# A hand-placed gated mixer kernel with a new order of all operations on every engine

## The chip, the cores and the metric

One Trainium2 chip, one core. The metric is device time in microseconds (us) of one launch. The kernel before took 224.87 us, the median of three runs (223.43 to 225.10).

## The reference

Two branches share the input `q` (2048 rows of 640, bf16) and are mixed by a gate per row:

```python
g = sigmoid((x * gate_w).sum(-1))                 # one number per row
k_shift = 4-tap causal filter of k;  kv = k_shift * v
y = causal convolution of kv with ssm_k (length 2048, per channel; by FFT)
a = q * (y + kv * ssm_D)
h  = gelu(layernorm(x) @ w1)                      # 640 -> 640
x1 = x + shift_rows(h) @ w2                       # four column groups shifted by +1, -1, +2, -2 rows
b  = x1 + gelu(layernorm(x1) @ w3) @ w4           # 640 -> 1536 -> 640
out = g * a + (1 - g) * b
```

## The kernel before

The program first records 1176 operations with their operands and memory regions (class `Prog`), and then issues them in an order that is written out by hand as a list. An **operation** here is one instruction of VectorE (DVE), ScalarE (ACT) or GpSimd, one DMA, or one group of matmuls into a PSUM bank; it is named by its number in the recording. Three literals in the main function steer all of it:

- `SEQUENCE` is the order of the 1176 numbers. Each engine takes its own operations in that order, and so does each DMA queue: the queue of SyncE (SP) for loads, stores and transposing DMAs, the queue of GpSimd for DMAs that add into their target.
- `PLACES` gives the PSUM bank of each of the 206 matmul results.
- `ON` is a string of 151 bits. `turn(default)` flips the engine of one operation where its bit is "1": ScalarE or VectorE for copies and scalings, a DMA or VectorE for 32-row copies and for some additions.

`emit` walks the order, and before an operation waits on a semaphore for each operation whose result (or whose memory) it needs, also for an earlier one of the same engine, TensorE apart. Nothing is reordered at run time, so an engine whose next operation isn't ready stands still.

The parts of the work, by the functions that record them:

- `x_load`, `ln1`: load 16 row tiles; mean and variance with two `bn_stats` per tile (L847) and `bn_aggr` (L848); GpSimd raises the variance to the power -0.5 (`pool_pow`, L855); VectorE normalises; TensorE or a transposing DMA turns the tile.
- `mm1`, `mmg`: first matmul with gelu on ScalarE; 32-row pieces are copied to shifted places (L932), 24 in all.
- `mm2`, `ln2`: second matmul; VectorE adds the residual out of PSUM (L966); statistics, the power on GpSimd again, a normalising pass per tile (on ScalarE or VectorE by `turn`), a transposing DMA.
- `mm3`, `base`, `mm4`: the 1536-wide pair of matmuls, in four blocks of 512 rows; its result is added into the output by DMAs on GpSimd's queue.
- For each of five channel chunks c: `h_load`, `h_fold`, `h_even`, `h_chunk` take the filter to its spectrum HF; `k_load`, `v_load`, `kv`, `kv2`, `x_fwd`, `combine` take the signal to XF; `unit` multiplies the two spectra block by block. `unit` is VectorE's largest part: multiplications and additions over 1024 or 2048 elements in each of 128 partitions (L646); fourteen of the additions are done by DMAs that add.
- `final`: inverse transform by matmuls, flip, gating and the last additions.

Helper lines in the profile: L646 is every two-input VectorE operation (`tt`), L651 every one-input one (`ts`), L656 every ScalarE pass (`act`), L678 nearly every matmul (`mm`), L237 and L234 the plain and the transposing DMAs, L852 the small three-input operations. So a row is told apart by its shape.

Of the kernel before, what the change touches and what calls it, by code (L numbers as in the profile page):

```python
# [433 lines left out]
def bass_gated_mix__ssm_conv_h3__mixer_s_mlp__prompt_kernel(  # L434
    nc, A_q, A_k, A_v, A_shift_k, A_ssm_k, A_ssm_D, B_x, B_w1, B_w2, B_w3, B_w4, gate_w, out,
):
    S, D, F = 2048, 640, 1536
# [3 lines left out]
    P = Prog(nc)  # L441
# [27 lines left out]
    def ps(n, cls):  # L469
# [3 lines left out]
    SEQUENCE = [2, 4, 27, 1, 24, 7, 0, 5, 3, 8, 46, 53, 9, 10, 11, 45, 52, 12, 13, 14, 49, 15, 50, 16, 17, 25, 18,  # L473
# [66 lines left out]
    ON = ("0000000011111111111111111011011100110100010000101111000000000000011000000000110100000001010010001101"  # L540
          "001000010100001000100000000000000000000000000000000")
# [608 lines left out]
```

## Time and profile before

| | us |
|---|---|
| three runs | 224.87, 223.43, 225.10 |
| span of the profiled execution, first to last instruction | 222.3 |
| VectorE: first instruction, end of the last one | 0.82, 219.5 |
| last store lands, end of the span | 222.3 |

The profile is of one execution; its span is 1.1 to 2.8 us below the three runs, which also hold what lies around the span. A row of groups gives the line, engine and operation, the shape written and read, the count, then busy time in us and the mean duration of one in ns, then the idle time of the engine just before them. A row of the timeline gives start, length, engine, line, operation and count; the idle time before it, with what ended it, stands in brackets. Starts and lengths of neighbours on VectorE overlap by some 80 ns, so what one instruction costs is less than its duration.

### The profile page before, as it was taken

The numbers are of one execution on the slowest core, as the hardware profiler recorded it, in microseconds if no ns is written. First come the engines' busy times: TensorE is split into PE (matmuls) and PEld (weight loads), VectorE is DVE, ScalarE is ACT, GpSimd is POOL, SyncE is SP. The second block draws the span as 40 slices with busy tenths as digits, with TensorE's granted clock in tenths as the row PEclk, the third lists the DMA queues.
The fourth block names the chain that finished last, engine by engine and source line by source line (L and its number), as shares of the span: only waits on it lengthen the run. The fifth ranks groups of instructions, "written<-read, shape, count | busy, mean of one in ns | idle before, by whom it ended". The sixth has DMA issues, their size and how long they took to land.

```text
span 222.3 us, 3842 instructions
## 1 busy us (share of the span) xinstructions
PE 210.2 (95%) x1403; PEld 125.7 (57%) x1410; DVE 211.8 (95%) x417; ACT 193.4 (87%) x324; POOL 53.5 (24%) x57
## 2 busy tenths in 40 slices
PE   5999989799999999999999999999999999999971
PEld 2588755344675444665445575445666444677650
DVE  6999999899999979999999999999998999999994
ACT  2389999799999999899999999999987698666891
POOL 0422303200003300005140003034015416287431
PEclk9999999999999999999999999999999999999997
DMA  5997999999999999939958874599699959979895
GB/s 166 344 299 181 213 208 246 169 253 190 147 361 212 321 226 172 200 78 189 233 108 146 200 153 94 119 174 184 142 226 138 232 77 265 200 100 96 110 161 112
DMA packets 80561, 41.39 MB, mean 186 GB/s; under 512 B 59129, under 2 KB 77086, under 8 KB 80542
## 3 DMA queue, kind: packets, MB, share of 16 engines
q1 hardware_dynamic: 73872, 31.89, 64.9%
q0 software_dynamic: 6496, 9.18, 26.7%
q8 instruction: 11, 0.18, 0.3%
q10 hardware_dynamic: 174, 0.07, 0.1%
q14 instruction: 8, 0.07, 0.1%
HBM read 14.88 MB, written 5.77 MB: 93 GB/s over the span
## 4 chain that ended last, share of the span: by engine, by line
DVE 65%; PE 13%; ACT 11%; DMA 7%; issue 2%; ACTq 0%
DVE arena L646 59%; ACT arena L656 11%; PE PSall L678 10%; DMA arena<-arena 7%; PE PSall L701 3%; DVE arena L651 2%; DVE arena L932 1%; DVE arena L847 1%; DVE arena L966 1%; PE PSall L908 0%; DVE arena L852 0%; DVE arena L698 0%; DVE arena L848 0%; PE PSall L731 0%; DVE arena L689 0%
## 5 line engine op out<-in xcount | busy, mean ns | idle before, releaser
L678 PE MATMUL PSall<-arena 128*128 128x512 bf16 (+5 forms) x1342 | 202.0, 309 | 4.9 <-DVE arena L646 2.2
L646 DVE TENSOR_TENSOR arena<-arena 128x1024 bf16<-128x1024 bf16 (+13 forms) x266 | 173.4, 712 | 4.1 <-DMA arena<-arena 2.7
L678 PEld LDWEIGHTS PSall<-arena 128*128 128x128 bf16 x1349 | 121.4, 98 | 85.1 <-ACT arena L656 6.7
L656 ACT ACTIVATE arena<-PSall 128x512 bf16<-128x512 f32 (+6 forms) x157 | 93.4, 666 | 10.7 <-PE PSall L736 4.9
L656 ACT ACTIVATE arena<-arena 128x640 bf16<-128x640 bf16 (+5 forms) x105 | 90.7, 892 | 4.5 <-DVE arena L646 4.2
L855 POOL TENSOR_TENSOR arena<-arena 128x2 f32<-128x2 f32 (+2 forms) x15 | 17.1, 1145 | 87.6 <-DVE arena L852 71.4
L237 POOL DMA_DIRECT2D out_dram<-arena x24 | 25.5, 1285 | 15.1 <-DVE arena L646 8.9
L656 ACT ACTIVATE arena<-PSall,arena 128x640 bf16<-128x640 f32 (+2 forms) x32 | 20.4, 655 | 8.5 <-PE PSall L678 8.4
L237 POOL DMA_DIRECT2D arena<-arena x14 | 12.4, 882 | 61.1 <-DVE arena L646 61.1
L966 DVE SCALAR_TENSOR_TENSOR arena<-PSall,arena 128x640 bf16<-128x640 f32 x16 | 12.9, 814 | 0.5 <-PE PSall L678 0.5
L651 DVE TENSOR_SCALAR arena<-arena 128x640 bf16<-128x640 bf16 (+6 forms) x37 | 13.2, 376 | 0.1
L847 DVE BATCH_NORM_STATS2 arena<-arena 128x6 f32<-128x320 bf16 x20 | 8.8, 479 | 1.1 <-DMA arena<-in_A_q_dram 1.0
L701 PE MATMUL PSall<-arena 128*128 128x512 bf16 x15 | 6.4, 586 | 2.2 <-DVE arena L698 2.2
L932 DVE TENSOR_SCALAR arena<-arena 32x256 bf16<-32x256 bf16 (+1 forms) x23 | 5.5, 237 | 0.6 <-ACT arena L656 0.3
L656 ACT ACTIVATION_READ_ACCUMULATOR arena<-arena 128x1 f32 x28 | 5.8, 206 | 0.0
L701 PEld LDWEIGHTS PSall<-arena 128*128 128x128 bf16 x15 | 1.9, 136 | 5.0 <-issue 2.8
L908 PE MATMUL PSall<-arena 128*128 128x128 bf16 x40 | 3.4, 220 | 0.1
L852 DVE SCALAR_TENSOR_TENSOR arena<-arena 128x2 f32<-128x2 f32 (+2 forms) x19 | 3.0, 157 | 0.2 <-ACT arena L656 0.2
L908 PEld LDWEIGHTS PSall<-arena 128*128 128x128 bf16 x40 | 2.5, 98 | 0.5 <-DVE arena L651 0.2
L704 ACT ACT_TABLE_LOAD x1 | 1.3, 1283 | 1.3 <-PEq L1135 1.3
L848 DVE BATCH_NORM_AGGREGATE arena<-arena 128x2 f32<-128x12 f32 x10 | 1.8, 199 | 0.0
L966 DVE DVE_READ_ACCUMULATOR arena<-PSall,arena 128x1 f32 x16 | 1.3, 79 | 0.0
(19 smaller groups left out, 2.9 us busy)
## 6 DMA issues: line engine op xcount, KB each, us to landing
arena<-arena POOLq DMA_DIRECT2D x9, 512.0 KB, 6.5
arena<-in_A_ssm_k_dram SPq DMA_DIRECT2D x5, 512.0 KB, 4.2
arena<-in_A_q_dram SPq DMA_DIRECT2D x6, 320.0 KB, 5.7
arena<-in_B_w_dram SPq DMA_DIRECT2D x1, 1920.0 KB, 10.5
out_dram<-arena SPq DMA_DIRECT2D x16, 96.0 KB, 2.9
out_dram<-arena POOLq DMA_DIRECT2D x16, 96.0 KB, 4.7
arena<-in_A_q_dram SPq DMA_DIRECT2D x8, 192.0 KB, 3.3
out_dram<-arena POOLq DMA_DIRECT2D x8, 192.0 KB, 4.2
```

What stands on the lines that cost most here:

```text
L237: fn = lambda e: e.dma_start(out, in_, **kw)
L646: P.op(eng, lambda e: e.tensor_tensor(o, real(a), real(b), op), [a, b], [o], dve_ns(o, [a, b], 2) if eng == "dve" else 500)
L651: P.op(eng, lambda e: e.tensor_scalar(o, real(a), s1, s2, op0=op0, **({} if op1 is None else {"op1": op1})), [a] + aps, [o], dve_ns(o, [a] ...
L656: P.op("act", lambda e: e.activation(real(o), real(a), f, bias=bias, scale=scale, **({"accum_out": accum} if accum is not None else {})), ...
L678: fns.append(lambda e, l=l, r=r, i=i: e.matmul(real(o), l, r, start=(i == 0), stop=(i == last)))
L701: P.op("pe", lambda e: e.matmul(real(pw), warm[:, 0:128], warm[:, 128:640], start=True, stop=True), [warm], [pw], 427.0 if i < 14 else 216.0)
L847: P.op("dve", lambda e, o=o, i=i: e.bn_stats(o, i), [i], [o], 400)
L852: P.op("dve", lambda e: e.scalar_tensor_tensor(o, a, x, b, op0=op0, op1=op1), [a, b] + aps, [o], n_of(o) / 0.96 + 65)
L855: P.op("pool", lambda g: g.tensor_tensor(o, a, e, ALU.pow), [a, e], [o], dur)
L908: P.op("pe", [lambda e, c=c, pb=pb, xn=xn: e.transpose(real(pb)[:, 128 * c:128 * (c + 1)], xn[:, 128 * c:128 * (c + 1)], ident) for c in r ...
L932: P.op("dve", lambda e, o=hT[q, 4, c0:c0 + n], i=hx[q, :]: e.tensor_scalar(o, i, 1.0, None, op0=ALU.mult), [hx[q, :]], [hT[q, 4, c0:c0 + n ...
L966: P.op("dve", lambda e: e.scalar_tensor_tensor(x, real(pr), 1.0, x, op0=ALU.mult, op1=ALU.add, accum_out=st[1, 0][:, t:t + 1]), [pr, x], [ ...
```

## The change

All three literals are replaced: another `SEQUENCE` of the same 1176 operations, other `PLACES`, and `ON` with eleven bits changed. Two of the small clearing operations (L692, L694) name a wider region as their output in the recording; the instructions stay the same. The note on the change reads: laid out with longer GpSimd powers and later landings. These are figures that the order was worked out with; no such figure is part of the program.

What the eleven bits move (number, part, engine before, engine after):

| operation | before | after |
|---|---|---|
| 301, a filter tap of `kv(0)`, 128x2048 | ACT | DVE |
| 402, a copy of `h_even(2)`, 1x1024 | ACT | DVE |
| 518, 522 (`ln2(0,4)`) and 544, 545, 547 (`ln2(4,8)`), normalising passes, 128x640 | ACT | DVE |
| 129, gate sums of `mmg(0)`, 128x4 | ACT | DVE |
| 269, a 32-row copy of `mm1(3)`, 32x512 | DMA (SP) | DVE |
| 768, an addition of `unit(3)`, 128x2048 | DMA (GpSimd) | DVE |
| 815, a copy of `unit(4)`, 1x512 | DVE | ACT |

Moves of place that the prediction speaks of:

- SP's queue starts 46, 45, 47, 48, 130 before and 46, 45, 47, 130, 48 after (46, 45, 47, 48 load one 160 KB tile of x each, 130 loads two, 320 KB).
- GpSimd's queue has 542 (power of `ln2(4,8)`), 637, 640 (adding DMAs of `unit(0)`) before, and 637, 542, 640 after.
- The copies and additions of `h_even(2)` (400, 402) stand 5 us of VectorE work later, TensorE's `h_chunk(2)` (416, 417) at the same place among the matmuls.

```diff
-    SEQUENCE = [2, 4, 27, 1, 24, 7, 0, 5, 3, 8, 46, 53, 9, 10, 11, 45, 52, 12, 13, 14, 49, 15, 50, 16, 17, 25, 18,
...
+    SEQUENCE = [27, 46, 8, 28, 45, 26, 1, 5, 4, 3, 2, 0, 9, 47, 10, 25, 11, 130, 12, 24, 13, 48, 31, 32, 52, 131,
...
-    ON = ("0000000011111111111111111011011100110100010000101111000000000000011000000000110100000001010010001101"
-          "001000010100001000100000000000000000000000000000000")
+    ON = ("0000000001111111111111111111011110110110010000100110111000000000011000000000110100000001010010001100"
+          "001000010100001000000000000000000000000000000000000")
...
-    P.op("dve", lambda e: e.memset(hT[0:32, 4, 2:3], 0.0), [], [hT[0:32, 4, 2:3]], 70)
+    P.op("dve", lambda e: e.memset(hT[0:32, 4, 2:3], 0.0), [], [hT[0:32, 4, 2:4]], 70)
...
-    P.op("dve", lambda e: e.memset(hT[32:64, 4, S + 1:S + 2], 0.0), [], [hT[32:64, 4, S + 1:S + 2]], 70)
+    P.op("dve", lambda e: e.memset(hT[32:64, 4, S + 1:S + 2], 0.0), [], [hT[32:64, 4, S:S + 2]], 70)
```

More of the change, by code (lines that the diff above doesn't have):

```diff
@@ L471, in ps @@
         return v if n == 1 else v.rearrange("p (b n) -> p b n", b=2)
-    SEQUENCE = [2, 4, 27, 1, 24, 7, 0, 5, 3, 8, 46, 53, 9, 10, 11, 45, 52, 12, 13, 14, 49, 15, 50, 16, 17, 25, 18,
[59 rows of a table removed]
-    PLACES = [2, 4, 7, 0, 4, 5, 6, 1, 2, 1, 3, 4, 2, 3, 3, 4, 2, 6, 7, 2, 0, 4, 5, 7, 6, 2, 6, 1, 0, 7, 4, 1, 6, 0,
[6 rows of a table removed]
-    ON = ("0000000011111111111111111011011100110100010000101111000000000000011000000000110100000001010010001101"
-          "001000010100001000100000000000000000000000000000000")
+    SEQUENCE = [27, 46, 8, 28, 45, 26, 1, 5, 4, 3, 2, 0, 9, 47, 10, 25, 11, 130, 12, 24, 13, 48, 31, 32, 52, 131,
[59 rows of a table added]
+    PLACES = [0, 1, 3, 7, 2, 4, 5, 0, 2, 3, 3, 0, 5, 0, 6, 6, 6, 5, 7, 2, 7, 7, 1, 6, 6, 0, 4, 0, 5, 1, 5, 4, 2, 0,
[6 rows of a table added]
+    ON = ("0000000001111111111111111111011110110110010000100110111000000000011000000000110100000001010010001100"
+          "001000010100001000000000000000000000000000000000000")
     HW = S + 4
```

130 rows, old and new, of tables (PLACES, SEQUENCE) are left out of this document.

## The prediction, made before the result was known

> **What bounds the kernel now.** I read the engines' busy shares first, then the chain of waits that ended last, then the busy time by stretches.
>
> ```profile
> PE 210.2 (95%) x1403; PEld 125.7 (57%) x1410; DVE 211.8 (95%) x417; ACT 193.4 (87%) x324; POOL 53.5 (24%) x57
> ...
> DVE 65%; PE 13%; ACT 11%; DMA 7%; issue 2%; ACTq 0%
> ```
>
> ```profile
> 68.00:86.00 18.00, 17.95 (x88) 8.40 (x88) 16.62 (x25) 17.79 (x25) 3.87 (x3) 1.00 1.04 250
> 86.00:122.00 36.00, 35.85 (x212) 20.54 (x213) 35.93 (x53) 35.06 (x50) 6.65 (x5) 1.00 0.82 159
> 122.00:163.00 41.00, 40.95 (x246) 23.96 (x246) 40.97 (x59) 39.76 (x57) 6.86 (x8) 1.00 0.79 156
> 163.00:207.00 44.00, 43.74 (x272) 26.23 (x271) 42.70 (x62) 33.28 (x56) 21.54 (x24) 1.00 0.97 162
> ```
>
> The columns of the second view are the stretch, its length, and the busy time of TensorE, its weight loads, VectorE, ScalarE and GpSimd. VectorE and TensorE are both nearly full; ScalarE has room only after 163 us. The chain goes through VectorE for 65% of the span. A matmul's end is modelled, so TensorE's 17.95 of 18 may hide small waits; VectorE's gaps are true ones, and these are all that were longer than 0.15 us:
>
> ```profile
> 3.18 1.67 DVE L847 BATCH_NORM_STATS2 arena<-arena 128x6 f32<-128x320 bf16 x4 [1.00 <-DMA arena<-in_A_q_dram]
> 15.21 0.22 DVE L932 TENSOR_SCALAR arena<-arena 32x256 bf16<-32x256 bf16 x1 [0.28 <-ACT arena L656]
> 41.89 0.16 DVE L852 SCALAR_TENSOR_TENSOR arena<-arena 128x4 f32<-128x4 f32 x1 [0.18 <-ACT arena L656]
> 43.22 0.69 DVE L646 TENSOR_TENSOR arena<-arena 128x1024 bf16<-128x1024 bf16 x1 [0.45 <-DMA arena<-arena]
> 52.19 1.31 DVE L646 TENSOR_TENSOR arena<-arena 128x16 f32<-128x16 f32 x2 [0.18 <-ACT arena L656]
> 64.33 0.82 DVE L966 SCALAR_TENSOR_TENSOR arena<-PSall,arena 128x640 bf16<-128x640 f32 x1 [0.53 <-PE PSall L678]
> 67.57 1.23 DVE L646 TENSOR_TENSOR arena<-arena 128x2047 bf16<-128x2047 bf16 x1 [0.45 <-ACT arena L656]
> 82.22 1.55 DVE L646 TENSOR_TENSOR arena<-arena 128x2048 bf16<-128x2048 bf16 x2 [1.38 <-DMA arena<-arena]
> ...
> 170.49 36.72 DVE L646 TENSOR_TENSOR arena<-arena 128x2048 bf16<-128x2048 bf16 x52 [0.89 <-DMA arena<-arena]
> ```
>
> They sum to 5.34 us. So VectorE is the bound: it works almost without a break from 3.2 us to its end, and all that a better order alone can win here is 5.3 us less the first load.
>
> **The change, part by part.** First what VectorE has to do. Of the eleven flipped operations ten come to VectorE and one leaves it. Their prices:
>
> ```profile
> L646 DVE TENSOR_TENSOR arena<-arena 128x2048 bf16<-128x2048 bf16 x56 | 66.8, 1216 | 2.5 <-DMA arena<-arena 2.3
> L651 DVE TENSOR_SCALAR arena<-arena 128x640 bf16<-128x640 bf16 x16 | 6.8, 430 | 0.1
> L651 DVE TENSOR_SCALAR arena<-arena 128x2048 bf16<-128x2048 bf16 x6 | 4.4, 748 | 0.0
> L932 DVE TENSOR_SCALAR arena<-arena 32x512 bf16<-32x512 bf16 x7 | 2.0, 286 | 0.1
> L651 DVE TENSOR_SCALAR arena<-arena 1x512 bf16<-1x512 bf16 x1 | 0.3, 274 | 0.0
> ```
>
> ```profile
> 41.97 0.80 DVE L651 TENSOR_SCALAR arena<-arena 128x640 bf16<-128x640 bf16 x2
> ...
> 48.62 1.41 DVE L651 TENSOR_SCALAR arena<-arena 128x2048 bf16<-128x2048 bf16 x2
> ```
>
> Two taps of 0.75 us take 1.41 together, two normalising passes of 0.44 take 0.80: a neighbour starts 0.08 us before the one in front of it ends, so an instruction costs its duration less 0.08. Operation 301 then costs 0.66; the five normalising passes 5 x 0.36 = 1.78; the addition 768 costs 1.22 - 0.08 = 1.14; the 32-row copy 269 costs 0.29 - 0.08 = 0.21; 815, which leaves, gives back 0.19. Two shapes have no row. The 1x1024 copy lies between the 1x512 copy (0.19) and the full 2048 pass (0.66); I take 0.38, twice the shorter, since it has twice the elements. The four gate sums lie between nothing and 0.25 (they read PSUM, as the 0.81 us additions of L966 do with 640 elements); I take 0.07. Sum: 0.66 + 1.78 + 1.14 + 0.21 + 0.38 + 0.07 - 0.19 = 4.05 us, with bounds 3.8 and 4.6.
>
> An instruction that needs the one just in front of it does not overlap. In the chain of waits such a pair looks like this:
>
> ```profile
> 189.09 0.02 issue
> 189.12 1.24 DVE arena L646
> ```
>
> The start is 0.02 to 0.03 us after the end of the one in front instead of 0.08 before it, so 0.11 us are lost. Counting neighbours in both written orders gives 16 such pairs before and 13 after: 0.35 us less. The 32-row copies break the overlap too; changes between 32-row groups number 36 in both orders, so they add nothing. **VectorE's work grows by 3.7 us.** ScalarE loses eight passes and gains one; on VectorE that can shorten only the four waits on ScalarE above.
>
> The Trainium skill (VectorE: DVE Perf Modes, "The DRAIN you can't avoid") says that a semaphore between two VectorE operations costs nothing extra, because the pipe drains anyway. By that the 0.35 us would not be saved and the sum below would end 0.35 us higher. The rows above differ (0.08 us of overlap without a wait, none with one), and the measurement decides.
>
> Next the loads at the start. Tile 48 now stands behind the 320 KB of 130 on SP's queue.
>
> ```profile
> L237 SPq DMA_DIRECT2D arena<-in_A_q_dram x1: 432/432/432, 2.1 to 2.1; - x1
> ...
> DMA to landing us min/median/max: 4.0/4.0/4.0
> ```
>
> ```profile
> L237 SPq DMA_DIRECT2D arena<-in_A_q_dram x1: 452/452/452, 2.6 to 2.6; - x1
> ...
> DMA to landing us min/median/max: 4.9/4.9/4.9
> ```
>
> 48 landed at 6.1 us, 130 at 7.5. With the two swapped the same bytes have to pass before 48 is there, so it lands at 7.5. On VectorE 48's statistics come after those of tile 47 (landed 5.3, two at 0.42) and two small operations (0.36), at 6.5 us: a wait of 1.0 us. The old order lost 0.1 on 130 there, so this costs 0.9, with bounds 0 (if landings do not follow the queue) and 1.2.
>
> Then the old waits. The 0.89 us at 170 us ended with the adding DMA 768; the addition is now VectorE's own, and is priced above. The 1.38 us at 82.2 ended with the adding DMA 637, which took 8.9 us to land:
>
> ```profile
> 73.33 1.07 POOL L237 DMA_DIRECT2D arena<-arena  x1 [1.72 <-DVE arena L646]
> 77.08 0.88 POOL L237 DMA_DIRECT2D arena<-arena  x1 [2.68 <-DVE arena L646]
> ```
>
> Between the last product that it adds and its reader lay 7.9 us of VectorE work, and now lie 11.8: gone, with 3 us to spare. The matmuls behind the 0.53 at 64.3 stand 4 us earlier on TensorE. The readers behind the waits on ScalarE (0.28, 0.18, 0.18, 0.45) stand 2.7 to 13 us of VectorE work later, while ScalarE has less in front of them. I let these seven go: 3.89 us. The 0.45 at 43.2 stays, since the room before it is 6.38 us and was 6.41; the first load stays.
>
> Last, new waits. Along the new order I added up VectorE's work between each producer and its reader. It is tight in few places: the readers of adding DMAs in `unit(3)` and `unit(4)` have 0.3 and 0.5 us less room than before and would just wait; the powers of the first tiles are read 0.2 us after they should be done. I take 0.6 us for all of it, with bounds 0 and 3.
>
> **Sum**, against the profiled execution: 222.3 + 3.7 + 0.9 - 3.9 + 0.6 = 223.6 us of span, 0.6% more. The runs shown have a median of 224.87 for this span of 222.3; scaled alike the forecast is **226.2 us**. What a measurement of this kernel can tell from no change is about 1%, here 222.6 to 227.1.
>
> **Rivals.**
>
> *TensorE takes over (slower).* `h_chunk(2)` keeps its place among the matmuls, but what it reads comes later: the additions of `h_even(2)` stand 5.0 us of VectorE work later, and the row copy 402, done on ScalarE at 82.2, follows them on VectorE.
>
> ```profile
> 81.20 1.04 ACT L656 ACTIVATE arena<-arena 1x1024 bf16<-1x1024 bf16 x1
> ```
>
> ```profile
> 85.53 1.24 PE L678 MATMUL PSall<-arena 128*128 128x512 bf16 x5
> ```
>
> The row at 82.22 above holds the last of these additions to matter (400), which ends at 83.8; operation 416 is the third matmul of the last row, at 86.0, so it stood 2.2 us behind. In the new order TensorE reaches 416 two matmuls (0.4 us) earlier. With VectorE at its old pace TensorE stops there for 5.0 + 0.4 (the copy) + 0.4 - 2.2 = 3.6 us. After that the stretches leave it 0.5 us of idle time until 207. If it regains nothing, all later products are 3.6 us late: 222.3 + 3.6 = 225.9, **228.5 us**. It decides where the stop is longer than what VectorE lost elsewhere: I expect VectorE to have dropped some 2 us of its old waits by then, which makes the stop 1.5 us, and matmul ends are modelled, so some idle time is hidden in 17.95 of 18. Against it speaks also that VectorE itself is 3.7 us longer, so that TensorE has that much time.
>
> *GpSimd's queue (slower).* The adding DMA 640 now stands behind the power 542, and that waits for an operation 541 of VectorE that comes 3.2 us of VectorE work after 640's own data.
>
> ```profile
> 69.69 1.92 POOL L855 TENSOR_TENSOR arena<-arena 128x4 f32<-128x4 f32 x1 [26.41 <-DVE arena L852]
> ...
> 100.41 3.15 POOL L855 TENSOR_TENSOR arena<-arena 128x4 f32<-128x4 f32 x1 [22.45 <-DVE arena L852]
> ```
>
> ```profile
> DMA to landing us min/median/max: 8.0/8.0/8.0
> ```
>
> From 541 to the reader of 640 lie 9.0 us of VectorE work; the power (1.92) and the old landing (8.0) need 9.9: a wait of 0.9, and 2.1 if the power takes 3.15 as it did once. Against it: 640 landed slowly while 1920 KB of weights were under way, which by then have landed. With 2.1 the span is 225.7, **228.3 us**.
>
> The Trainium skill (SBUF — State Buffer, "Who interferes with whom") says that a two-input VectorE operation and a GpSimd operation that reads SBUF exclude each other, the later one standing still; by it a power among long additions takes long, and this case takes its longer form. The two rows of one shape, 1.92 and 3.15 us, agree that the same power can take more.
>
> *Only the waits count.* If the loads land in time in spite of the swap, the 0.45 goes too and nothing new comes, the span is 222.3 + 3.7 - 3.9 - 0.4 = 221.7, **224.3 us**: no change. This is the floor within 0.9 us, since even with none of the 5.34 us of gaps the span is 220.7 (223.2).
>
> **How the numbers follow.** Forecast 0.52, TensorE 0.17, GpSimd 0.11, only waits 0.20. The likeliest case alone spans 224.5 to 227.8. Faster by over 1% would need a span under 220.1, below the floor; only the spread of the runs can give it: 0.06, out of the case of waits. Slower by over 1%: nearly all of the two slower rivals (0.27) and the upper edge of the forecast (0.06), 0.33. Within 1%: 0.61. The range reaches from the floor to the dearer rival: 223.4 to 229.0.
>
> **What would show it.** VectorE's busy time near 215.5 us, with ScalarE's lower; the first statistics waiting twice, 1.0 us each; no gap at the readers of 637 and 768; adding DMAs thirteen instead of fourteen. VectorE's gaps together should be near 3 us. The forecast is wrong if VectorE's busy time grows by less than 3 us, or if its gaps sum to more than 5: then the row that ends them says which rival holds (TensorE after 86 us; an adding DMA near 90).

## The result, and the profile after

The changed kernel takes 227.36 us, the median of nine runs (226.38 to 228.99); the kernel before, beside it, 224.87 us (nine runs, 223.43 to 226.05). The ratio is 1.0128, 95% interval 1.0093 to 1.0164: slower by 1.3% (the medians alone give 1.1%), 1.1 us above the forecast and inside its range, but past the band within 1% that the prediction held likeliest (0.61). The profiled execution is the slowest of the nine, 228.99 us with a span of 227.2; the nine spans run from 224.6 to 227.2, with a median of 225.5. Executions of e2 and e3 (two of the experiments below) with a lower granted TensorE clock (0.976 to 0.981 of full speed) ran 1.6 to 3.7% longer than the fastest of their kernel and are left out of the ratios below, and the profiles of e2 and e3 are of such executions, so only single waits are read from them.

Busy time of the engines after, and the shares of the chain that ended last:

```profile
PE 212.9 (94%) x1402; PEld 127.8 (56%) x1410; DVE 215.5 (95%) x426; ACT 188.7 (83%) x317; POOL 53.4 (24%) x56
...
PE 68%; DVE 19%; DMA 4%; ACT 2%; issue 2%; POOL 1%; ACTq 1%
```

VectorE's busy time is the 215.5 us that was forecast. But the chain, which went through VectorE for 65% before, now goes through TensorE for 68%. The busy time by stretches, with the same columns and stretches as before:

```profile
68.00:86.00 18.00, 17.95 (x96) 9.28 (x96) 17.88 (x34) 15.66 (x23) 3.33 (x3) 1.00 0.90 259
86.00:122.00 36.00, 35.84 (x204) 19.94 (x205) 35.90 (x53) 35.05 (x52) 8.15 (x8) 1.00 0.95 184
122.00:163.00 41.00, 40.90 (x245) 23.91 (x246) 40.97 (x62) 38.91 (x54) 11.04 (x11) 1.00 0.91 161
163.00:207.00 44.00, 43.95 (x274) 26.55 (x274) 43.65 (x64) 36.40 (x60) 12.90 (x14) 1.00 0.78 142
```

VectorE's waits after 68 us are gone but for one of 0.21 us (17.88 of 18 in the first stretch, where it had 16.62), and now both engines are full from there on. All of VectorE's waits longer than 0.15 us, from its timeline:

```profile
3.08 1.67 DVE L847 BATCH_NORM_STATS2 arena<-arena 128x6 f32<-128x320 bf16 x4 [1.14 <-DMA arena<-in_A_q_dram]
...
5.46 0.89 DVE L847 BATCH_NORM_STATS2 arena<-arena 128x6 f32<-128x320 bf16 x2 [0.27 <-DMA arena<-in_A_q_dram]
...
7.28 0.89 DVE L847 BATCH_NORM_STATS2 arena<-arena 128x6 f32<-128x320 bf16 x2 [0.53 <-DMA arena<-in_A_q_dram]
...
16.83 0.22 DVE L932 TENSOR_SCALAR arena<-arena 32x256 bf16<-32x256 bf16 x1 [3.49 <-ACT arena L656]
...
181.88 1.22 DVE L646 TENSOR_TENSOR arena<-arena 128x2048 bf16<-128x2048 bf16 x1 [0.21 <-ACT arena L656]
```

One wait makes up most of it: 3.49 us before 16.83, for a gelu of ScalarE. Behind it stands TensorE's start, after and then before:

```profile
1.59 2.31 PE L701 MATMUL PSall<-arena 128*128 128x512 bf16 x5 [1.59 <-DVE arena L698]
6.02 0.29 PE L731 MATMUL PSall<-arena 5*128 5x5 bf16 x4 [2.11 <-DMA arena<-cI]
6.24 4.02 PE L701 MATMUL PSall<-arena 128*128 128x512 bf16 x9
10.05 0.74 PE L908 MATMUL PSall<-arena 128*128 128x128 bf16 x5
```

```profile
2.24 5.30 PE L701 MATMUL PSall<-arena 128*128 128x512 bf16 x12 [2.24 <-DVE arena L698]
7.47 0.21 PE L736 MATMUL PSall<-arena 5*128 5x5 bf16 x2
7.61 0.67 PE L701 MATMUL PSall<-arena 128*128 128x512 bf16 x2
8.12 0.44 PE L908 MATMUL PSall<-arena 128*128 128x128 bf16 x5
```

L701 are warm-up products that need no input; L731 are the four small products of operation 39 (the taps), which need the identity `cI`; L908 is the first turned tile. Before, 39 stood behind all fifteen warm-up products and after the first turned tile. Now it stands behind five, the identity isn't there, and nine more warm-up products, which need nothing, stand behind it: TensorE idles 2.11 us and the first turned tile comes at 10.05 in place of 8.12. The identity is late because its load has moved on ScalarE's DMA queue:

```profile
0.74 0.57 ACTq L237 DMA_DIRECT2D arena<-in_A_ssm_D_dram  x1
1.34 0.27 ACTq L237 DMA_DIRECT2D arena<-in_gate_w_dram  x1
1.64 0.31 ACTq L237 DMA_DIRECT2D arena<-in_A_shift_k_dram  x1
1.98 0.39 ACTq L237 DMA_DIRECT2D arena<-cI  x1
...
10.83 0.77 ACT L656 ACTIVATE arena<-PSall 128x640 bf16<-128x640 bf16 x2 [6.93 <-PE PSall L908]
```

It is fourth, issued at 1.98, and its view gives 4.0 us from issue to landing; before it was second, at 1.41, with 2.5 us. ScalarE then waits 6.93 us for its first turned tile, and VectorE for ScalarE.

The Trainium skill (PSUM — Partial Sum Buffer, "Engine vs sequencer instructions") says that matmuls start and complete in program order. The trace agrees: nine products without a need of their own stood 2.11 us behind four that waited.

The identity is not the whole of the 3.49 us. The run e7 below has the same start, and TensorE waits even longer in it (2.54 us), yet VectorE's wait there is 1.94. The products behind it show the difference, the changed kernel's first, then e7's:

```profile
11.59 1.25 PE L678 MATMUL PSall<-arena 128*128 128x128 bf16 x10 [0.65 <-ACT arena L656]
```

```profile
12.02 0.73 PE L678 MATMUL PSall<-arena 128*128 128x128 bf16 x10 [0.66 <-ACT arena L656]
```

In the changed kernel TensorE still runs slow there. The trace's record of its granted clock begins, at full speed, at 15.1 us in this execution, at 11.1 in e7 and at 7.8 in the kernel before; the matmuls before that time are the long ones. From the first turned tile to VectorE's row at 16.83 it takes 6.8 us, in e7 5.4. So some 1.4 us of the 3.49 belong to this execution, the slowest of the nine.

### The profile page after: what moved, and what is told of

Its sections match the earlier page's. It is cut to its first block, busy times and chain, and to the rows that moved or that the text cites. A ratio compares the mean times of both kernels' runs of the same rounds, so it can differ in the third digit from the quotient of the medians.

```text
span 227.2 us, 3840 instructions
## 1 busy us (share of the span) xinstructions
PE 212.9 (94%) x1402; PEld 127.8 (56%) x1410; DVE 215.5 (95%) x426; ACT 188.7 (83%) x317; POOL 53.4 (24%) x56
## 4 chain that ended last, share of the span: by engine, by line
PE 68%; DVE 19%; DMA 4%; ACT 2%; issue 2%; POOL 1%; ACTq 1%
PE PSall L678 66%; DVE arena L646 11%; DVE arena L966 3%; DMA arena<-arena 3%; ACT arena L656 2%; DVE arena L651 2%; DVE arena L932 2%; PE PSall L701 2%; DMA arena<-cI 2%; POOL arena L855 1%; PE PSall L908 1%; ACTq L237 1%; DVE arena L847 0%; DVE arena L852 0%; PE PSall L731 0%
## 5 line engine op out<-in xcount | busy, mean ns | idle before, releaser
L646 DVE TENSOR_TENSOR arena<-arena 128x1024 bf16<-128x1024 bf16 (+10 forms) x267 | 174.7, 715 | 0.8 <-ACT arena L656 0.2
L678 PEld LDWEIGHTS PSall<-arena 128*128 128x128 bf16 x1349 | 122.7, 98 | 86.2 <-ACT arena L656 4.5
L656 ACT ACTIVATE arena<-arena 128x640 bf16<-128x640 bf16 (+5 forms) x99 | 83.7, 869 | 5.2 <-DVE arena L646 2.5
L855 POOL TENSOR_TENSOR arena<-arena 128x2 f32<-128x2 f32 (+2 forms) x15 | 17.8, 1188 | 75.6 <-DVE arena L852 54.7
L237 POOL DMA_DIRECT2D arena<-arena x13 | 11.9, 914 | 65.7 <-DVE arena L646 63.9
L651 DVE TENSOR_SCALAR arena<-arena 128x640 bf16<-128x640 bf16 (+6 forms) x43 | 16.2, 396 | 0.3
L701 PE MATMUL PSall<-arena 128*128 128x512 bf16 x15 | 7.0, 631 | 1.6 <-DVE arena L698 1.6
L701 PEld LDWEIGHTS PSall<-arena 128*128 128x128 bf16 x15 | 1.9, 141 | 4.4 <-issue 2.7
L908 PE MATMUL PSall<-arena 128*128 128x128 bf16 x40 | 4.2, 248 | 0.0
L908 PEld LDWEIGHTS PSall<-arena 128*128 128x128 bf16 x40 | 3.2, 114 | 0.9 <-issue 0.5
L731 PE MATMUL PSall<-arena 5*128 5x5 bf16 x4 | 0.3, 174 | 2.1 <-DMA arena<-cI 2.1
L731 PEld LDWEIGHTS PSall<-arena 5*128 5x128 bf16 x4 | 0.2, 114 | 3.0 <-DMA arena<-cI 3.0
```

The source lines that it names most:

```text
L237: fn = lambda e: e.dma_start(out, in_, **kw)
L646: P.op(eng, lambda e: e.tensor_tensor(o, real(a), real(b), op), [a, b], [o], dve_ns(o, [a, b], 2) if eng == "dve" else 500)
L651: P.op(eng, lambda e: e.tensor_scalar(o, real(a), s1, s2, op0=op0, **({} if op1 is None else {"op1": op1})), [a] + aps, [o], dve_ns(o, [a] ...
L656: P.op("act", lambda e: e.activation(real(o), real(a), f, bias=bias, scale=scale, **({"accum_out": accum} if accum is not None else {})), ...
L678: fns.append(lambda e, l=l, r=r, i=i: e.matmul(real(o), l, r, start=(i == 0), stop=(i == last)))
L701: P.op("pe", lambda e: e.matmul(real(pw), warm[:, 0:128], warm[:, 128:640], start=True, stop=True), [warm], [pw], 427.0 if i < 14 else 216.0)
```

## The experiments

Two questions: is the start the cost, or the ten operations that VectorE took over; and which engine sets the end. Ratios are against the kernel before in the same session, with 95% intervals. VectorE's waits are those over 0.15 us after its first load, in the profiled execution; e9's profile, like the changed kernel's, is of its slowest execution. In the edits of the order below a line holds only the numbers of the queue or engine that it is about; in the literal others stand between them.

| kernel | ratio | VectorE busy, us | its waits, us |
|---|---|---|---|
| before | 1 | 211.8 | 4.3 |
| changed | 1.0128 (1.0093 to 1.0164) | 215.5 | 4.5 |
| e1, identity first | 1.0067 (1.0029 to 1.0105) | 215.4 | 0.4 |
| e9, taps later | 1.0057 (1.0032 to 1.0082) | 215.7 | 2.2 |
| e11, before, with the late start | 1.0060 (1.0029 to 1.0092) | 211.7 | 5.9 |
| e2, new order, old engines | 1.0476 (1.0413 to 1.0539) | 211.8 | 15.9 |
| e3, old order, new engines | 1.0201 (1.0141 to 1.0260) | 216.5 | 8.0 |
| e4, less TensorE | 1.0118 (1.0077 to 1.0160) | 215.2 | 2.5 |
| e7, less VectorE | 1.0166 (1.0123 to 1.0209) | 211.2 | 7.8 |
| e10, both less | 1.0070 (1.0033 to 1.0108) | 210.9 | 5.8 |
| e13, e1 with less VectorE | 1.0044 (1.0008 to 1.0080) | 211.2 | 4.8 |
| e12, e1 with both less | 0.9974 (0.9948 to 0.9999) | 210.9 | 4.0 |
| e14, e1 with both less, earlier | 0.9936 (0.9914 to 0.9959) | 211.9 | 2.0 |
| e6, e1 with copies by DMA | 1.0132 (1.0103 to 1.0162) | 213.2 | 4.6 |

### The start: e1, e9, e11

e1 changes only the order of four loads on ScalarE's queue (25 is the identity):

```diff
-27, 28, 26, 25
+25, 26, 27, 28
```

> The changed order with one thing different: on ScalarE's queue the load of the identity matrix (25) stands first instead of fourth. Theory (VectorE is the bound, and the change lost 3.5 us on it at 13 us because TensorE stood still for the identity): TensorE's wait of 2.1 us at 3.9 us goes, VectorE's wait of 3.5 us at 13 us falls to about 1.4, and the time falls from 227.4 to about 225.4 us. Rival (the lost time at the start is regained later anyway, because TensorE or something else sets the end): the wait falls, the time stays within 0.5 us of 227.4.

e9 leaves the loads and moves the taps on TensorE behind the warm-up products:

```diff
-9, 10, 11, 12, 13, 39, 14, 15, 16, 17, 18, 19, 20, 21, 22, 60
+9, 10, 11, 12, 13, 14, 15, 16, 17, 18, 19, 20, 21, 22, 39, 60
```

> The changed order with one thing different: the small matmuls for the taps (39), which need the identity, stand behind the warm-up matmuls, just before the first turned tile (60), as they do in the old order; the identity still loads fourth. Theory (the taps, placed early, make TensorE stand still for the identity, and the warm-up matmuls behind them then delay the first turned tile): TensorE has no wait for the identity, VectorE's wait at 13 us is under 1 us, the time is 225.2 us like that of the run with the identity first. Rival (the wait comes from the loads of x or from ScalarE's late table load): the wait stays over 1.5 us, the time stays near 227.4.

e11 goes the other way: the kernel before with the identity fourth and the taps behind five warm-up products, in a free bank (24 is ScalarE's table load, which moves behind the four loads as well, as in the changed kernel; the lines of its helpers are one higher).

```diff
-27, 24, 25, 28, 26
+27, 28, 26, 25, 24
...
-9, 10, 11, 12, 13, 14
+9, 10, 11, 12, 13, 39, 14
```

> The kernel before with the start of the changed one alone: the identity's transfer issued fourth on ScalarE's queue, the four small products of the taps put behind five of the warm-up products (with a PSUM bank of their own), nothing else. If the loss at the start is what the change costs and it is carried to the end in any order, the first turned tile comes at about 10 us in place of 8.1 and the time rises by 1.5 to 3 us, to 225.7 to 227.2 us. If the kernel before has slack that takes it up (its VectorE waits of 3.9 us in all, its 0.45 us at 43 us), the time stays within 0.7 us of 224.2 us.

Measured: e1 225.19 us, e9 225.22 us, e11 225.96 us against 224.34 for the kernel before beside it. All three times came out as the start's theory had it. In e1 the wait is gone altogether, where 1.4 us of it had been expected to stay; this is all that VectorE waited for, grouped by what ended it:

```profile
DVE arena L847 <- DMA arena<-in_A_q_dram: 1.5, 2, 1.3
DVE arena L698 <- PEq L1135: 0.9, 1, 0.9
DVE arena L646 <- ACT arena L656: 0.2, 1, 0.2
```

The columns are the sum, the number and the longest. From 5.5 us to its end at 220.0 VectorE has one wait of 0.2. In e11 the same loss appears in an order that didn't have it (TensorE, then VectorE):

```profile
6.12 0.29 PE L732 MATMUL PSall<-arena 5*128 5x5 bf16 x4 [1.58 <-DMA arena<-cI]
```

```profile
14.55 0.22 DVE L933 TENSOR_SCALAR arena<-arena 32x256 bf16<-32x256 bf16 x1 [1.63 <-ACT arena L657]
```

So the pair (identity fourth, taps early) costs by itself: 1.3 us by ratio (1.6 by medians) put into the kernel before, 1.4 us taken out of the changed one (0.0061 of 224). It is carried to the end in other company too: e13 lies 2.7 us under e7 and e12 2.2 us under e10, pairs that differ in nothing else. What is left of the change is 0.6 to 0.7%.

The break in the warm-up products does more than stop TensorE for its own length: it delays the full clock. The record of full clock begins at 9.4 to 15.1 us in the six profiled executions with the late identity and the early taps (the changed kernel, e2, e4, e7, e10, e11), and at 5.0 to 7.8 us in the other eight. Moving one of the two back brings it forward (7.5 us in e1, 5.0 in e9), and putting both into the kernel before delays it from 7.8 to 11.0 (e11).

The wait varies from one execution to the next: five kernels share the start (the changed one, e4, e7, e10, e2), and their profiled executions show it at 3.49, 2.05, 1.94, 1.45 and 2.15 us. The changed kernel's profile caught the longest. That this makes the spread of its nine runs is likely, but only one of the nine has a profile.

### Half of the change: e2, e3

e2 is the new order with the old engine bits, e3 the old order with the new bits:

```diff
-    ON = ("0000000001111111111111111111011110110110010000100110111000000000011000000000110100000001010010001100"
+    ON = ("0000000011111111111111111011011100110100010000101111000000000000011000000000110100000001010010001101"
...
```

> The changed order, but the eleven operations stay on their old engines. Theory (VectorE's 3.7 us of added work are paid in full): 227.4 - 3.7 + 0.9 (the addition 768 is again awaited) = 224.6 us, VectorE busy near 211.8. Rival (TensorE sets the end from 66 us on): VectorE's work falls and its gaps grow by as much, the time stays near 227.4.

> The old order, but the eleven operations on their new engines. Theory (work on VectorE is paid in full): 224.9 + 3.7 - 0.9 (the wait for 768) = 227.7 us. Rival (TensorE sets the end): near 224.9. It also tells whether the order by itself won or lost anything: the changed kernel is at 227.4.

Both expectations failed: e2 costs 4.8%, far more than the whole change, and e3 2.0%, above the 1.2% that its theory gave (its interval overlaps that of the whole change). In e2 VectorE has no more work than before, but stands still, for ScalarE, which has its passes back, and for an adding DMA:

```profile
101.68 1.23 DVE L646 TENSOR_TENSOR arena<-arena 128x2048 bf16<-128x2048 bf16 x1 [3.67 <-ACT arena L656]
...
180.70 2.48 DVE L646 TENSOR_TENSOR arena<-arena 128x2048 bf16<-128x2048 bf16 x2 [3.37 <-DMA arena<-arena]
```

The last is the reader behind the adding DMA 768. In e3 the reader behind an adding DMA of `unit(0)` (640, issued at 78.3) waits likewise:

```profile
90.63 2.50 DVE L646 TENSOR_TENSOR arena<-arena 128x1024 bf16<-128x1024 bf16 x4 [3.87 <-DMA arena<-arena]
```

So here order and engine bits can't be priced apart: the new order loses with the old engines, and the old order with the new ones.

### Which engine sets the end: e4, e7, e13

The prediction took VectorE for the bound. e4 leaves out 64 of TensorE's products, all after 90 us (forecast as 8.5 us; TensorE's busy time falls by 6.5 where nothing else differs, 210.7 in e13 and 204.2 in e12); e7 takes 4.3 us from VectorE, between 164 and 182 us.

```diff
-(uT[:, c, 128 * i:128 * (i + 1)], w4[:, c, lo:hi]) for c in range(FC)]
+(uT[:, c, 128 * i:128 * (i + 1)], w4[:, c, lo:hi]) for c in range(FC - 2)]
```

> The changed kernel with two of the twelve pieces of the last matmul's sum left out (10 of 12 in mm4), which takes 16 x 2 x 0.267 = 8.5 us of matmuls from TensorE after 90 us and nothing from VectorE. Theory (VectorE is the bound): within 1 us of 227.4. Rival (TensorE sets the end): 2 to 6 us less.

```diff
-                        tt(acc[i], acc[i], tmp[i], ALU.add)
+                        w = slice(0, 16 if c == 3 else 512)
+                        tt(acc[i][:, :, w], acc[i][:, :, w], tmp[i][:, :, w], ALU.add)
```

> The changed kernel with VectorE's six additions of unit(3) done on 16 of every 512 columns only, so part of the sum is left out: three of 1.14 us and three of 0.60 us shrink to about 0.1 each, 4.7 us of VectorE's work near 170 us. Theory (VectorE is the bound there): the time falls by 4 to 4.7 us, to about 223. Rival (TensorE, which has almost no idle time there, sets the end): less than 1.5 us.

e4 gave 226.26 us, e7 227.82: against the changed kernel's 1.0128 neither is a gain. e13 repeats e7's edit without the bad start:

> The identity's transfer issued first, and only VectorE's cut (4.3 us less; most of the fourth unit's additions are left out). With the identity first VectorE ran without a gap from 5.5 to 220 us, so if it alone is the bound there, as the prediction had it, this gives 221 to 222 us. If TensorE, which was dense from 62 us on, is the second wall, VectorE's cut turns into gaps and the time stays at 224.5 to 225.7 us.

It gave 225.23 us, and its span of 223.3 is e1's 223.4 with 4.3 us less of VectorE's work. The chain that ended last shows why, and VectorE's timeline where the time went:

```profile
62.23 145.44 PE PSall L678 x861
```

```profile
170.92 5.71 DVE L646 TENSOR_TENSOR arena<-arena 128x1536 bf16<-128x1536 bf16 x12 [2.68 <-ACT arena L656]
178.16 1.23 DVE L646 TENSOR_TENSOR arena<-arena 128x2048 bf16<-128x2048 bf16 x1 [1.54 <-ACT arena L656]
```

In this chain 861 matmuls follow each other for 145 us without a stop. VectorE comes earlier to what TensorE has not yet made, and waits 2.68 and 1.54 us for ScalarE's copies of its products. The theory that VectorE alone is the bound fell with e7 and e13. The rival that TensorE alone is it had 2 to 6 us for e4, which gained 0.2 by ratio; the two intervals, taken together, leave room for some 1.5 at most.

The Trainium skill (Perfetto Trace Analysis, "Identifying the Most-Contended Engine") says to take the engine with the highest occupancy and to optimise it first; for TensorE's headroom it goes not by the matmuls' share but by their work and by the share of the weight loads, 56% here. By the matmuls' share or the weight loads', that is VectorE, 95% against TensorE's 94% or 56%, and 4.3 us less work on it gained nothing that can be told. Here the measurement decides against reading one engine off the shares; the page's next section, "Optimization Strategy", does say that the most contended engine can change over a kernel.

### Both at once: e10, e12, e14

If two engines are each full, only relieving both helps. e10 joins the edits of e4 and e7; e12 does so on e1.

> The changed kernel with two cuts at once: the sums of the third product of each block row take 10 of 12 pieces (about 8.5 us less of TensorE's work, all after 90 us), and the six VectorE additions of the fourth unit take 16 of 512 columns (about 4.3 us less of VectorE's). What is left out: two of twelve pieces of those sums and most of that unit's additions. Each cut alone gave nothing that could be told from the changed kernel's 227.4 us (226.3 and 227.8). If TensorE and VectorE are both walls, each dense to the end, the two cuts together give what neither gave: 222.5 to 224.5 us, with VectorE and TensorE both idle less than 4 us more than before in the stretch from 90 us on. If something else holds the end (ScalarE, the transfers, the order of the banks), the two together give no more than one: 226 to 228 us, and the idle time shows up on both engines at once.

> The same two cuts, and the identity's transfer issued first of ScalarE's (which by itself gave 225.2 us). What is left out: as in the run with both cuts. If two walls and the start add up, each term keeps its size: about 2 us under the run with both cuts, 220.5 to 222.5 us. If the start's loss is only felt while an engine is dense to the end, the cuts have made slack that swallows it, and the time is that of the run with both cuts within 0.7 us.

e10 gave 226.03 us, e12 224.01: 1.3 and 2.1 us under the changed kernel and e1 by ratio (0.0058 and 0.0093), but only a third to a half of the 4.3 us taken from VectorE. e10's gain is only just clear of noise (its interval overlaps that of the changed kernel); its time lies just inside its rival's range (226 to 228), not in the theory's. e12's forecast missed too, while the step between the two (about 2 us) held. One pair is clear: e12 differs from e13 in TensorE's cut alone and is 0.0070 lower, 1.6 us, with intervals that don't meet. So TensorE's cut pays when VectorE has less to do. VectorE's cut on top of TensorE's (e10 against e4) is 0.0048, inside the intervals, and TensorE's cut alone on e1 was not run. The stretches of e12 show where the relief didn't meet:

```profile
110.00:160.00 50.00, 47.69 (x269) 25.71 (x268) 49.97 (x74) 47.37 (x67) 15.88 (x16) 1.00 0.85 162
160.00:170.00 10.00, 9.07 (x58) 5.29 (x57) 8.24 (x13) 8.93 (x13) 1.73 (x2) 1.00 0.91 168
170.00:180.00 10.00, 9.92 (x55) 5.06 (x53) 8.21 (x16) 8.37 (x13) 2.59 (x3) 1.00 0.83 181
```

From 110 to 160 us TensorE is free for 2.3 us while VectorE is full; from 170 to 180 TensorE is full and VectorE free for 1.8; only between are both free. The two cuts lay mostly in different stretches. e14 lays VectorE's cut on the second unit (`c == 1` in e7's edit, 112 to 131 us), where TensorE's cut is felt:

> The identity first, TensorE's sums cut to 10 of 12 pieces, and VectorE's cut laid on the second unit (its six additions on 16 of 512 columns, 114 to 131 us) in place of the fourth: so both cuts lie in the stretch from 90 to 160 us, where the run with both cuts left TensorE idle 0.8 to 1 us in 20 and VectorE without a gap. What is left out: two of twelve pieces of those sums and most of that unit's additions. The cut in the fourth unit lay from 168 to 182 us, where TensorE was dense again and VectorE waited 2.2 and 1.2 us for ScalarE's copies of TensorE's products; that is why it gave little, if TensorE and VectorE are the only walls. Then here the time falls by 3 to 4 us under the 225.2 us of the identity first alone, to 221 to 222.2 us (ratio to before 0.988 to 0.993). If ScalarE, busy 19.1 to 19.8 of 20 us there, is a third wall, or if the dense stretch of TensorE after 160 us sets the end by itself, the gain is at most 1.5 us: 223.7 us or more (ratio 0.997 or more), with VectorE waiting for ScalarE or TensorE before 170 us.

It gave 222.90 us, 0.9936 of the kernel before and 2.9 us under e1 by ratio. Its span fell by 2.5 us for 3.6 us less on VectorE, and two new waits on ScalarE came:

```profile
123.09 3.65 DVE L646 TENSOR_TENSOR arena<-arena 128x2048 bf16<-128x2048 bf16 x5 [0.74 <-ACT arena L656]
...
130.96 2.36 DVE L646 TENSOR_TENSOR arena<-arena 128x2048 bf16<-128x2048 bf16 x2 [0.80 <-ACT arena L656]
```

The result lies between the two expectations, by ratio just above the first (0.993). It fits two full engines in the same stretch; ScalarE, busy 19.8 of 20 us between 110 and 130 us in this run, is close behind as a third. Neither VectorE's cut in the second unit nor TensorE's was run alone on e1, so how much of the 2.9 us needs both is open: that both are needed is argued from e13 and e4, not shown here.

### A try at a better version: e6

On e1, eight of the 32-row copies go from VectorE to DMAs on SP's queue (226 to 229 and 267 to 270), and two clearing operations go to the start: 2.2 us less on VectorE.

> The run with the identity first, and eight of the 32-row copies of mm1 (226 to 229 and 267 to 270, 32x512) done by DMAs on SP's queue instead of VectorE, and the two clearing operations 6 and 7 moved to the start. It takes 8 x 0.29 us and the breaks of overlap around them from VectorE, some 3 us, and puts eight DMAs of 0.5 us into SP's queue in two places, ahead of v_load(1) and of the transpose of kv(1). Theory (VectorE is the bound and has no gaps in that run): the time falls from 225.2 by 2.5 to 3 us to about 222.5, below the kernel before (224.5). Rival (the DMAs land too late, and the matmuls of mm2 or the later loads make VectorE wait for as long): 225 or more.

It gave 227.19 us, 0.65% more than e1, and its rival held: the copies wait on SP's queue for their data, and the loads behind them come late.

```profile
53.03 1.23 DVE L646 TENSOR_TENSOR arena<-arena 128x2048 bf16<-128x2048 bf16 x1 [1.53 <-DMA arena<-in_A_v_dram]
55.46 0.69 DVE L646 TENSOR_TENSOR arena<-arena 128x1016 bf16<-128x1016 bf16 x1 [1.21 <-DMA arena<-in_A_ssm_k_dram]
```

TensorE then idles 1.34 and 1.29 us for VectorE at 59.4 and 62.2. No version that computes everything was faster than the kernel before.

## Why the prediction was right or wrong

- **VectorE's work, +3.7 us: right.** 211.8 to 215.5. The rule of 0.08 us of overlap, and 0.11 us per dependent pair, held in sum to 0.1 us; its parts were not measured one by one. The two guessed shapes came out close: the 1x1024 copy lasts 0.41 us, so it costs 0.33 (0.38 was taken), the gate sums 0.16, so 0.08 (0.07).
- **The first loads, +0.9 us: right in sum.** Three waits of 1.14, 0.27 and 0.53, 1.94 in all, against 1.00; not two of 1.0 each. In e1, with the same loads on SP's queue, they are 1.32 and 0.17, so the size varies between executions.
- **Seven old waits go, -3.9 us: right.** All seven went (none of them is left in e1 either), and the one at 43.2 (0.45) that was to stay went too. Neither reader of 637 or 640 waits, and thirteen adding DMAs were issued.
- **New waits, +0.6 us with bounds 0 and 3: this is the step that failed.** It measured 3.7 in the profiled execution: 3.49 and 0.21. I added up VectorE's work between producer and reader, and so looked only at rooms measured on VectorE. The late producer was several steps away: the place of a 64 KB load on ScalarE's queue, a product waiting for it on TensorE, nine products behind it, the first turned tile, ScalarE's gelu. That TensorE would stay slow for longer after such a break had no term either. I priced the queue of SP that the text of the change touched, but not ScalarE's queue or the start of TensorE's order, which moved too. The profile is of the slowest run, 1.7 us of span above the median; in four other kernels with this start the wait is 1.45 to 2.15 us. That it was as small in the median run, and that the time missed by 1.1 us only for this reason, is likely but not shown.
- **That the time lies inside the range is partly luck.** The forecast's own case (224.5 to 227.8) holds it because it left up to 3 us for new waits, but the wait that came was none of those that it had in view. Its middle, 0.6%, is what is left without the bad start (0.6 to 0.7% in e1 and e9); that these two sizes agree does not show that VectorE's 3.7 us are the cause of what is left.
- **The ends: not priced.** VectorE begins 0.13 us later, and 0.56 us more lies behind its end. With it the span of the profiled execution closes: 222.34 + 3.71 + 0.43 (all gaps, 6.97 to 7.40) + 0.13 + 0.56 = 227.17, measured 227.16.
- **"VectorE is the bound": wrong as a statement of cause.** That sum is only an account of one full engine, and TensorE lost at the start as well: its busy time shows 7.29 of the first 10 us before and 6.30 after. e7 and e13 show that VectorE's work alone isn't what the end hangs on, and e4 that TensorE's alone isn't. The words that fail are "So VectorE is the bound": in the changed order TensorE stands right beside it. The cuts were made in the changed order only, so for the kernel before this is not shown.
- **The mark for being wrong, gaps over 5 us, was reached**: 5.6. The row that ends the gaps was to name a rival, and named neither: TensorE was not stopped at `h_chunk(2)` (17.95 of 18 between 68 and 86 us) and GpSimd's queue delayed no reader. The case of only the waits (224.3) fell, since something new came.
- Open: of the 0.6 to 0.7% that is left without the bad start, how much is VectorE's 3.7 us and how much TensorE's own order is not known. The one edit that gave VectorE less to do early (e6) brought waits of its own.

## What to carry to other kernels

When everything is reordered, follow the first input of each engine through every queue that issues it, ScalarE's among them: a needy product in front of work that needs nothing wastes the cover that this work was to give. Where two engines stand at 95% and 94%, as here, neither need be the bound by itself: a cut on one of them turned into waits, cuts on both in different stretches gave little, and cuts on both in the same stretch gave the most. An order and the engines it was laid out for belonged together here: trying one half told little of the whole.

## What had not been expected of the hardware

- A 64 KB load issued at 1.98 us as the fourth of ScalarE's queue took 3.4 to 4.4 us to land (seven kernels), as the second at 1.41 us 2.4 to 2.5 (two), and as the first at 0.74 us 2.3 (five). Whether the place or the time makes the difference was not tried.
- A wait of 1.6 to 2.5 us in the warm-up products, five products in, moved the start of TensorE's full clock from 5.0 to 7.8 us to 9.4 to 15.1 us.
- The chain of waits moved from 65% VectorE to 68% TensorE while their busy shares moved by one point (95 and 95, then 95 and 94). So here the chain, read alone, does not tell which of two full engines sets the end.
